# Diagonal score blocks: three quarters by matmuls, the fourth by a transposing DMA

## The chip, the core and the metric

The kernel runs on one core of one Trainium2 chip. That core has a matrix engine (TensorE, "PE" in the profile, with its weight loads shown apart as "PEld"), a vector engine (DVE), a scalar engine (ACT), GpSimd (POOL) and a queue engine (SyncE, "SP") that here issues every DMA. All DMAs of the kernel go through this one queue, in the order in which they stand there, and run on 16 DMA engines. The metric is device time in microseconds of one execution; the median of three timed runs of the kernel before is 1010.86 us (1010.35 to 1011.36).

## The reference

Two stages, on eight batches of 3136 rows:

```python
# gated attention, d_qk = 64, D = 256
scores = (1/S) * z @ z.T                 # S x S, S = 3136: symmetric
attn   = np.maximum(scores, 0.0) ** 2    # symmetric as well
x      = u * (attn @ v)
# low-rank mixer, rank 32, and a channel MLP, 256 -> 1024 -> 256
h   = x.transpose(0, 2, 1) @ U @ V
u2  = x + h.transpose(0, 2, 1)
out = u2 + np.maximum(u2 @ w_ch1, 0.0) @ w_ch2
```

The scores are a product of `z` with itself, so the block of rows J and columns g is the transpose of the block of rows g and columns J, and a block on the diagonal is its own transpose.

## The kernel before

**Tiling.** The 3136 rows of a batch are six groups of 512 rows (four tiles of 128) and one small group of 64. A score block is 512 keys by 512 queries; it is held in bf16 in one of 20 buffers (`blk0` to `blk19`) of 128 partitions by 4 x 512, with key tile `j` in columns `j*512` to `j*512+511`. For a batch there are 36 blocks. A block above the diagonal (J > g) is made once by matmuls and its mirror (rows g, columns J) is made from it by a transposing DMA. A block on the diagonal is made whole by matmuls. In batch 0 the groups 0 to 3 are an exception (`made_twice`, line 325): all of their blocks are made by matmuls.

**Making a block.** `score_pairs` (line 341) makes a block in two halves, `h` = 0 (key tiles 0 and 1) and `h` = 1 (key tiles 2 and 3). A half is a pair of matmuls, one on each half of TensorE's rows (contraction 64), each 128 keys by 512 queries, into two PSUM banks. The two matmuls of a pair run side by side. `score_finish` (line 387) has ACT or DVE apply scale and ReLU (`rectify`, line 309: one instruction of 128 x 1024, PSUM to `blk`, ACT at line 317, DVE at line 313) and then has DVE square it in place (`square`, line 307). For a block above the diagonal a transposing DMA becomes ready some time after the second square (`issue_turn`, line 328, DMA at line 333: 128 x 2048 in, 16 squares of 128 x 128 out). Among ready ones the one with the smallest J is issued first.

**Using it.** `av_stream` (line 493) runs `attn @ v` for group g over 24 key tiles, blocks 0 to 5 in order; the function `lhs` in it gives the 128 x 128 piece of a block that is the next weight. It is emitted as 96 pairs of matmuls of 256 columns, and everything else on TensorE (scores of the next group, the mixer and the MLP of a group one batch earlier) is placed between those pairs by `emit` (line 849).

**Order.** The program is written by hand, in one order, by a planner: `clock[0]` counts TensorE's work, `free_at` books ACT, DVE and the SP queue (34 units for a transposing DMA), and `hold` and `run_held` keep work until it is due by that count. So what a step costs in the planner decides where all later instructions stand on their queues. The items are the 56 (batch, group) pairs; item (b, g) runs `attn @ v` for it, makes the scores of the next group, and does the MLP of an item a batch earlier.

**The mixer's input.** For each group, `u2_unit` (line 653) makes `u2`, casts it to bf16 (`x_bf`) and has it transposed by a DMA of 128 x 1024 (`x_turn`, line 613, DMA at line 616) into `u2T`, which the first matmuls of `ch1_part` (line 745) read. This DMA stands on the same SP queue as the transposing DMAs of the score blocks, the loads of `u` (line 270), `v` (line 227) and `z` (lines 200, 205) and the stores of the output (line 824).

Of the kernel before, what the change touches and what calls it, by code (L numbers as in the profile page):

```python
# [18 lines left out]
def kernel(  # L19
# [11 lines left out]
    nc = tc.nc  # L31
# [5 lines left out]
    P = 128  # L37
# [7 lines left out]
    GW = GT * P  # L45
# [35 lines left out]
    squared = {}  # L81
    blocks = {}

    def take_block():
        k = free_blocks.pop(0)
        return k, pool.tile([P, GT, GW], BF16, name=f"blk{k}", bufs=1)
# [9 lines left out]
    clock = [0.0]  # L96
    free_at = {"act": 0.0, "dve": 0.0, "sp": 0.0}
    held = []
    unturned = {}
    ready_turns = []  # L100

    def book(eng, ready, cost):
        free_at[eng] = max(free_at[eng], ready) + cost
        return free_at[eng]

    def hold(due, f):
        held.append((due, len(held), f))

    def run_held(now=None):
        now = clock[0] if now is None else now  # L110
        while True:
            ripe = [h for h in held if h[0] <= now]
            if not ripe:
                break
            h = min(ripe, key=lambda e: (e[0], e[1]))
            held.remove(h)
            h[2]()
        while ready_turns and free_at["sp"] <= now:
            issue_turn(min(ready_turns, key=lambda e: (e[0], e[2], e[1])))

    def pe(cost):
        clock[0] += cost
# [3 lines left out]
    ps_free = [0.0] * NPS  # L126

    def take_ps():
        k = min(range(NPS), key=lambda i: ps_free[i])
        assert ps_free[k] < float("inf")  # L130
        clock[0] = max(clock[0], ps_free[k])
        ps_free[k] = float("inf")
        for bank in range(2):
            wrote.pop((k, bank), None)
        return k, ps_pool.tile([P, 2, GW], FP32, name=f"ps{k}")
# [23 lines left out]
    def pair(k, ops, n):  # L159

        if any(wrote.get((k, bank), (h,))[0] != h for h, bank, _ in ops):
            post(k)
        for h, bank, args in ops:
            ins = nc.tensor.matmul(**args)  # L164
            last = wrote.get((k, bank))
            if last and last[0] != h:
                behind(ins, last[2])
            wrote[k, bank] = [h, ins, None]
        pe(n / 256)
# [132 lines left out]
    def half(zzT, jj, c0, n):  # L302
        return zzT.rearrange("p t c -> p (t c)")[jj * dqk : (jj + 1) * dqk, c0 : c0 + n]

    def square(a, cost=6.3):
        book("dve", clock[0], cost)
        nc.vector.tensor_tensor(out=a, in0=a, in1=a, op=ALU.mult)  # L307

    def rectify(dst, src):

        ready = clock[0] + 3
        if max(free_at["dve"], ready) + 8 < max(free_at["act"], ready):
            nc.vector.tensor_scalar(  # L313
                out=dst, in0=src, scalar1=scale, scalar2=0.0, op0=ALU.mult, op1=ALU.max
            )
            return book("dve", ready, 11.2)
        nc.scalar.activation(out=dst, in_=src, func=AF.Relu, scale=scale)  # L317
        return book("act", ready, 8.7)

# [3 lines left out]
    def made_twice(b, g):  # L325
        return b == 0 and g <= FIRST

    def issue_turn(e):
        ready_turns.remove(e)
        J, g, b = e  # L330
        src = blocks[b, g, J]
        blocks[b, J, g] = take_block()
        nc.sync.dma_start_transpose(
            out=blocks[b, J, g][1].rearrange("p j (q c) -> p (j q) c", c=P),
            in_=src[1].rearrange("p j c -> p (j c)"),
        )
        book("sp", clock[0], 34)
        if unturned.pop(src[0]):
            free_blocks.append(src[0])

    def score_pairs(jobs):

        made = []
        for b, g, job in jobs:
            zzT = zzTs[b]
            k, ps = take_ps()
            if job == "last":
                keys, cols = [NF, NF], [groups[g + jj][0] for jj in range(2)]
            else:
                J, h = job  # L350
                keys, cols = [J * GT + 2 * h + jj for jj in range(2)], [groups[g][0]] * 2
            pair(
                k,
                [
                    (
                        jj,
                        jj,
                        dict(
                            out=ps[:, jj, :],
                            lhsT=half(zzT, jj, keys[jj] * P, P),  # L360
                            rhs=half(zzT, jj, cols[jj], GW),
                            start=True,
                            stop=True,
                        ),
                    )
                    for jj in range(2)
                ],
                GW,
            )
            if job == "last":  # L370
                lasts[b, g // 2] = pool.tile([P, 2, GW], BF16, name="last_sb")
                made.append((lasts[b, g // 2], k, ps, None, None))
                continue
            if h == 0:
                blocks[b, g, J] = take_block()
            made.append(
                (
                    blocks[b, g, J][1][:, 2 * h : 2 * h + 2, :],
                    k,
                    ps,  # L380
                    (J, g, b) if h == 1 and J > g and not made_twice(b, J) else None,
                    (b, g, J),
                )
            )
        return made

    def score_finish(made):
        for dst, k, ps, turn, key in made:
            if turn:
                J, g, b = turn  # L390
                unturned[blocks[b, g, J][0]] = False
            done = rectify(dst, ps)
            ps_free[k] = done

            def finish(dst=dst, turn=turn, key=key):
                square(dst)
                if key:
                    squared[key] = squared.get(key, 0) + 1
                if turn:
                    hold(clock[0] + 7, lambda: ready_turns.append(turn))  # L400

            hold(done, finish)

    def score_burst(jobs):
        score_finish(score_pairs(jobs))
# [87 lines left out]
    def av_stream(b, g, box):  # L493
        def lhs(h, q, jt):
            jb, j = divmod(jt, GT)
            while (b, jb) not in v_cast:
                if spare and not b:
                    spare.pop(0)()
                else:
                    run_held(min(h[0] for h in held))  # L500
            while (b, g, jb) not in blocks:
                if (g, jb, b) in ready_turns:
                    issue_turn((g, jb, b))
                else:
                    run_held(min(h[0] for h in held))
            t = blocks[b, g, jb][1]
            if jb >= g or made_twice(b, g):
                while squared.get((b, g, jb), 0) < 2:
                    run_held(min(h[0] for h in held))
                return t[h, j, q * P : (q + 1) * P]  # L510

            return t.rearrange("p a c -> p (a c)")[h, (q * GT + j) * P : (q * GT + j + 1) * P]

        per = 2 * GT

        def step(i, way, first, least):
            if first:
                xs[b, g] = pool.tile([P, GT, D], BF16, name="x_bf", bufs=8)
                box["k"], box["ps"] = take_ps()
            jt, a = divmod(i, 2)  # L520
            pair(
                box["k"],
                crossed(
                    way,
                    a,
                    lambda h, q: dict(
                        out=four(box["ps"])[:, q, :],
                        lhsT=lhs(h, q, jt),
                        rhs=v_bfs[b][h, jt, :],
                        start=first,  # L530
                        stop=False,
                    ),
                ),
                D,
            )
            while box.get("given", 0) < least // per:
                give_block(blocks[b, g, box.get("given", 0)])
                box["given"] = box.get("given", 0) + 1

        return Ways(2 * NF, 1, step, box)  # L540
# [487 lines left out]
    made = score_pairs(jobs_of(0, 0)[0:4])  # L1028
# [23 lines left out]
    for b in range(B):  # L1052
        for g in range(NQ):
            t = b * NG + g - 1
            new = jobs_of(b, g)
            if g == 0 and b > 0:
                x, y = (5, 10) if b == 1 else (5, 11)
# [14 lines left out]
    for t in range(n_items):  # L1072
# [45 lines left out]
        if av and full:  # L1118
# [5 lines left out]
            n = len(mine) - 3  # L1124
            qs += [(9 + 74 * i / n, 1, False, lambda: scores(1)) for i in range(n)]
        elif av:
# [5 lines left out]
            k = min(2, len(mine) // 3)  # L1132
            n = len(mine) - 3 * k
# [98 lines left out]
```

## Time and profile before

| what | value |
|---|---|
| timed runs, median | 1010.86 us (1010.35 to 1011.36) |
| the profiled execution: span from first to last instruction | 1010.2 us |
| TensorE: matmuls busy | 986.7 us, 98% of the span, 16171 matmuls |
| TensorE: weight loads busy | 776.4 us, 77% |
| DVE busy | 648.0 us, 64% |
| ACT busy | 517.3 us, 51% |
| mean granted TensorE clock | 0.997 of full speed |
| DMA queue of the kernel | 166.64 MB, 76.9% of 16 engines' span |
| transposing DMAs of score blocks | 114 (128 x 2048); beside them 55 for `u2T` and 7 for `zzT` |

The profile gives the span of its execution and no other time of it; the timed median lies 0.65 us above that span. The page's second part shows the same thing over time: TensorE's digit is 9 in every slice from the sixth to the 39th of 40 (some 25 us each) and lower only in the first, fourth, fifth and last, and the DMA row has 9 in six of the first fifteen slices. The other engines are well below full everywhere. A matmul's busy time is its latency and not the time for which it keeps the array, so pairs overlap; how long one pair keeps TensorE is read from the starts of runs of equal matmuls.

### The profile page before, as it was taken

How to read it: one execution, taken by the hardware profiler on the slowest of the kernel's cores; microseconds unless marked ns; L12 is line 12 of the kernel's file. 1: busy time of each engine (PE TensorE's matmuls, PEld its weight loads, DVE VectorE, ACT ScalarE, POOL GpSimd, SP SyncE). 2: the span in 40 equal slices, each digit the busy share in tenths (PEclk: the TensorE clock that was granted, in tenths of full speed). 3: DMA queues.
4: the chain of work that ended last, by engine and by line, in shares of the span. 5: the costliest groups of instructions: out<-in, count | busy, mean ns of one | idle time of the engine just before them, and what ended most of it. 6: DMA issues, size and time to landing. Idle time of an engine off the chain costs nothing.

```text
span 1010.2 us, 35325 instructions
## 1 busy us (share of the span) xinstructions
PE 986.7 (98%) x16171; PEld 776.4 (77%) x16171; DVE 648.0 (64%) x816; ACT 517.3 (51%) x595; POOL 17.1 (2%) x24
## 2 busy tenths in 40 slices
PE   5998899999999999999999999999999999999998
PEld 3897677777787777778777877778777777777776
DVE  4974675667656685666856677566776667653453
ACT  5885653357524574355733556434654356532453
POOL 4100000000000000000000000000000000000000
PEclk9999999999999999999999999999999999999999
DMA  7899997487976799558996689856799577953142
GB/s 242 166 249 225 218 203 165 127 171 176 224 149 159 140 204 214 150 150 174 183 215 165 130 184 190 216 127 140 179 209 191 138 152 128 180 127 88 45 103 94
DMA packets 341221, 168.89 MB, mean 167 GB/s; under 512 B 316496, under 2 KB 319568, under 8 KB 341072
## 3 DMA queue, kind: packets, MB, share of 16 engines
q1 hardware_dynamic: 341072, 166.64, 76.9%
q8 instruction: 126, 2.06, 0.9%
q14 instruction: 23, 0.19, 0.1%
HBM read 62.56 MB, written 25.69 MB: 87 GB/s over the span
## 4 chain that ended last, share of the span: by engine, by line
PE 94%; DMA 2%; ACT 1%; DVE 1%; POOL 0%; issue 0%; SPq 0%; POOLq 0%; ACTq 0%
PE ps L164 92%; PE ps L551 1%; DMA blk<-blk 1%; ACT blk L785 1%; PE ps L627 1%; DMA blk<-in_v_dram 1%; DVE blk L307 1%; ACT blk L317 1%; PE ps L835 0%; DMA u2T<-x_bf 0%; DVE blk L313 0%; POOL z_bf L213 0%; POOL v_bf L232 0%; DVE blk L822 0%; DVE x_bf L584 0%
## 5 line engine op out<-in xcount | busy, mean ns | idle before, releaser
L164 PEld LDWEIGHTS <-blk 64*128 64x128 bf16 x12288 | 611.0, 94 | 163.6 <-POOLq L154 8.8
L164 PE MATMUL ps<-v_bf,blk 64*128 64x256 bf16 x9216 | 617.2, 270 | 5.0 <-DMA blk<-blk 3.2
L317 ACT ACTIVATE blk<-ps 128x1024 bf16<-128x1024 f32 x321 | 320.7, 1028 | 342.0 <-PE ps L164 330.4
L307 DVE TENSOR_TENSOR blk<-blk 128x1024 bf16<-128x1024 bf16 x348 | 234.1, 698 | 42.2 <-ACT blk L317 41.6
L164 PE MATMUL ps<-u2T,w_bf 64*128 64x512 bf16 (+1 forms) x1792 | 237.8, 349 | 3.4 <-DMA u2T<-x_bf 2.7
L164 PE MATMUL ps<-w_bf,blk 64*128 64x256 bf16 x3072 | 193.5, 269 | 0.2
L782 DVE TENSOR_SCALAR blk<-ps 128x1024 bf16<-128x1024 f32 x94 | 113.3, 1205 | 100.0 <-PE ps L164 100.0
L785 ACT ACTIVATE blk<-ps 128x1024 bf16<-128x1024 f32 (+1 forms) x130 | 109.4, 850 | 82.4 <-PE ps L164 74.1
L164 PE MATMUL ps<-zzT 64*128 64x512 bf16 (+1 forms) x936 | 141.7, 343 | 1.7 <-ACT zzT L297 1.7
L164 PEld LDWEIGHTS <-w_bf 64*128 64x128 bf16 x1792 | 90.7, 94 | 34.6 <-POOLq L154 3.0
L584 DVE TENSOR_TENSOR x_bf<-ps,u_sb 128x1024 bf16<-128x1024 f32 x48 | 58.8, 1224 | 62.3 <-PE ps L164 62.3
L700 DVE TENSOR_TENSOR out_sb<-ps,x_bf 128x1024 f32<-128x1024 f32 (+1 forms) x49 | 54.3, 1107 | 53.4 <-PE ps L164 53.3
L822 DVE TENSOR_TENSOR out_sb<-ps,out_sb 128x1024 f32<-128x1024 f32 x42 | 51.3, 1222 | 18.3 <-PE ps L164 18.3
L164 PEld LDWEIGHTS <-zzT 64*128 64x128 bf16 x936 | 43.0, 95 | 9.3 <-ACT zzT L297 2.2
L317 ACT ACTIVATE last_sb<-ps 128x1024 bf16<-128x1024 f32 x23 | 23.6, 1024 | 26.1 <-PE ps L164 26.0
L313 DVE TENSOR_SCALAR blk<-ps 128x1024 bf16<-128x1024 f32 x23 | 28.2, 1225 | 13.4 <-PE ps L164 11.9
L186 DVE CAST x_bf<-out_sb 128x1024 bf16<-128x1024 f32 x34 | 23.4, 689 | 0.5
L164 PE MATMUL ps<-t_sb,V_bf 64*128 64x256 bf16 x200 | 20.7, 269 | 0.0
L186 DVE CAST v_bf<-stage 128x1024 bf16<-128x1024 f32 (+1 forms) x33 | 20.2, 611 | 0.0
L164 PE MATMUL ps<-v_bf,last_sb 64*128 64x256 bf16 x192 | 18.5, 269 | 0.0
L822 DVE TENSOR_TENSOR blk<-ps,blk 128x1024 f32<-128x1024 f32 x6 | 7.3, 1225 | 16.0 <-PE ps L164 15.9
L570 ACT COPY u_sb<-ps 64x512 f32<-64x512 f32 x8 | 4.7, 582 | 23.8 <-PE ps L551 23.8
(67 smaller groups left out, 248.6 us busy)
## 6 DMA issues: line engine op xcount, KB each, us to landing
u_sb<-in_u_dram SPq DMA_DIRECT2D x48, 512.0 KB, 5.0
stage<-in_v_dram SPq DMA_DIRECT2D x42, 512.0 KB, 6.0
out_dram<-out_sb SPq DMA_DIRECT2D x42, 512.0 KB, 3.1
stage<-in_z_dram SPq DMA_DIRECT2D x7, 512.0 KB, 5.7
blk<-in_v_dram SPq DMA_DIRECT2D x6, 512.0 KB, 7.3
out_dram<-blk SPq DMA_DIRECT2D x6, 512.0 KB, 2.6
blk<-in_moe_w_ch_dram SPq DMA_DIRECT2D x4, 512.0 KB, 6.6
blk<-blk SPq DMA_TRANSPOSE x114, 5.1
```

What stands on the lines that cost most here:

```text
L164: ins = nc.tensor.matmul(**args)
L186: nc.vector.tensor_copy(out=out, in_=in_)
L307: nc.vector.tensor_tensor(out=a, in0=a, in1=a, op=ALU.mult)
L313: nc.vector.tensor_scalar(out=dst, in0=src, scalar1=scale, scalar2=0.0, op0=ALU.mult, op1=ALU.max)
L317: nc.scalar.activation(out=dst, in_=src, func=AF.Relu, scale=scale)
L551: nc.tensor.matmul(out=ps[c * hp : c * hp + rows, h, :D], lhsT=smalls[b][h * hp : (h + 1) * hp, jt, :], rhs=v_bfs[b][h * hp : (h + 1) * hp ...
L584: nc.vector.tensor_tensor(out=xs[b, g][:rows, :n, :], in0=four(box["ps"])[:rows, :n, :], in1=u_sbs[b, g][:rows, :n, :], op=ALU.mult,)
L627: nc.tensor.matmul(out=pt[c * R : (c + 1) * R, 0, :D], lhsT=U_bf[:rows, it, :], rhs=xs[b, g][:rows, q, :], start=(it < NREP), stop=(it + N ...
L700: nc.vector.tensor_tensor(out=o[:rows, :n, :], in0=four(ps)[:rows, :n, :], in1=x, op=ALU.add)
L782: nc.vector.tensor_single_scalar(out=r, in_=ps[:, :, :gw], scalar=0.0, op=ALU.max)
L785: nc.scalar.activation(out=r, in_=ps[:, :, :gw], func=AF.Relu)
L822: nc.vector.tensor_tensor(out=o, in0=acc, in1=o, op=ALU.add)
```

## The change

A block on the diagonal is its own transpose. It is cut in quarters of two tiles by two tiles. The change makes the two quarters of key tiles 0 and 1, and the quarter of key tiles 2, 3 and query tiles 2, 3 by matmuls; the quarter of key tiles 2, 3 and query tiles 0, 1 is the transpose of the quarter of key tiles 0, 1 and query tiles 2, 3, and a transposing DMA of 128 x 512 makes it. So the first half (`h` = 0) is made by a pair of 512 columns as before, the second by a pair of 256 columns, and its ReLU and its square work on 512 columns per partition and not on 1024. The block's buffer keeps its size but holds the quarters in four runs of 512 columns: key tiles 0, 1 by queries 0, 1; the same by queries 2, 3 (what the DMA reads); key tiles 2, 3 by queries 2, 3; and what the DMA writes. `in_split` finds a piece there. This holds for all diagonal blocks but those that are `made_twice`: 2 in batch 0 and 6 in each of 7 batches, 44 in all.

The DMA becomes ready, by the planner, seven units after the first half's square, is booked with 12 units on the SP queue, and is chosen among the ready ones by the same rule as before (smallest J first). Where the stream of `attn @ v` comes to a piece of the fourth quarter and the DMA has not been placed yet, `lhs` places it then.

```diff
+    def split(b, g, J):
+        return J == g and not made_twice(b, g)
+    hw = GW // 2
+    def in_split(j, q):
+        if j < 2:
+            return (q // 2 * 2 + j) * hw + q % 2 * P
+        return 2 * GW + (j - 2) * hw + (q - 2) * P if q >= 2 else 3 * GW + (q * 2 + j - 2) * P
...
-            return book("dve", ready, 11.2)
+            return book("dve", ready, 11.2 if part == 1 else 6.4)
...
-        return book("act", ready, 8.7)
+        return book("act", ready, 8.7 if part == 1 else 5.3)
...
     def issue_turn(e):
         ready_turns.remove(e)
         J, g, b = e
         src = blocks[b, g, J]
+        if J == g:
+            nc.sync.dma_start_transpose(
+                out=flat_of(src)[:, 3 * GW :].rearrange("p (n c) -> p n c", c=P),
+                in_=flat_of(src)[:, GW : 2 * GW],
+            )
+            book("sp", clock[0], 12)
+            split_turned.add((b, g))
+            return
...
                 keys, cols = [J * GT + 2 * h + jj for jj in range(2)], [groups[g][0]] * 2
+                if split(b, g, J) and h:
+                    width = hw
+                    cols = [c + hw for c in cols]
...
-                            out=ps[:, jj, :],
+                            out=ps[:, jj, :width],
                             lhsT=half(zzT, jj, keys[jj] * P, P),
-                            rhs=half(zzT, jj, cols[jj], GW),
+                            rhs=half(zzT, jj, cols[jj], width),
...
+    def score_finish_split(flat, k, ps, h, key):
+        if h:
+            done = rectify(
+                flat[:, 2 * GW : 3 * GW].rearrange("p (j c) -> p j c", c=hw), ps[:, :, :hw], 0.5
+            )
+            a, cost = flat[:, 2 * GW : 3 * GW], 3.7
+        else:
+            done = rectify(
+                flat[:, : 2 * GW].rearrange("p (w j c) -> p j w c", w=2, j=2),
+                ps.rearrange("p j (w c) -> p j w c", w=2),
+            )
+            a, cost = flat[:, : 2 * GW], 6.3
+        ps_free[k] = done
+        def finish():
+            square(a, cost)
+            squared[key] = squared.get(key, 0) + 1
+            if not h:
+                b, g, J = key
+                hold(clock[0] + 7, lambda: ready_turns.append((J, g, b)))
+        hold(done, finish)
...
+                if split(b, g, jb):
+                    while j >= 2 and q < 2 and (b, g) not in split_turned:
+                        if (g, g, b) in ready_turns:
+                            issue_turn((g, g, b))
+                        else:
+                            run_held(min(h[0] for h in held))
+                    x = in_split(j, q)
+                    return t.rearrange("p a c -> p (a c)")[h, x : x + P]
                 return t[h, j, q * P : (q + 1) * P]
```

More of the change, by code (lines that the diff above doesn't have):

```diff
@@ L303, in half, with flat_of @@
         return zzT.rearrange("p t c -> p (t c)")[jj * dqk : (jj + 1) * dqk, c0 : c0 + n]
+    def split(b, g, J):
+        return J == g and not made_twice(b, g)
+    def flat_of(entry):
+        return entry[1].rearrange("p a c -> p (a c)")
+    hw = GW // 2
[3 more added lines that the diff above has]
+        return 2 * GW + (j - 2) * hw + (q - 2) * P if q >= 2 else 3 * GW + (q * 2 + j - 2) * P
     def square(a, cost=6.3):
@@ L307, in square, with rectify @@
         nc.vector.tensor_tensor(out=a, in0=a, in1=a, op=ALU.mult)
-    def rectify(dst, src):
+    def rectify(dst, src, part=1):
         ready = clock[0] + 3
-        if max(free_at["dve"], ready) + 8 < max(free_at["act"], ready):
+        if max(free_at["dve"], ready) + 8 * part < max(free_at["act"], ready):
             nc.vector.tensor_scalar(
@@ L315, in rectify @@
             )
-            return book("dve", ready, 11.2)
+            return book("dve", ready, 11.2 if part == 1 else 6.4)
         nc.scalar.activation(out=dst, in_=src, func=AF.Relu, scale=scale)
-        return book("act", ready, 8.7)
+        return book("act", ready, 8.7 if part == 1 else 5.3)
     def made_twice(b, g):
         return b == 0 and g <= FIRST
+    split_turned = set()
     def issue_turn(e):
@@ L346, in score_pairs @@
             k, ps = take_ps()
+            width = GW
             if job == "last":
@@ L367, in score_pairs @@
                 ],
-                GW,
+                width,
             )
@@ L375, in score_pairs @@
                 blocks[b, g, J] = take_block()
+            if split(b, g, J):
+                made.append((flat_of(blocks[b, g, J]), k, ps, h, (b, g, J)))
+                continue
             made.append(
@@ L388, in score_finish @@
         for dst, k, ps, turn, key in made:
+            if key and split(*key):
+                score_finish_split(dst, k, ps, turn, key)
+                continue
             if turn:
```

## The prediction

> **What bounds the kernel now.** I read the chain that ended last, then the stages, then TensorE's waits, then the queue that issues the DMAs. Chain and stages (columns: stretch, its length, busy time of PE, PEld, DVE, ACT, POOL, granted clock, DMA share, GB/s):
>
> ```profile
> PE 94%; DMA 2%; ACT 1%; DVE 1%; POOL 0%; issue 0%; SPq 0%; POOLq 0%; ACTq 0%
> ...
> 75.00:100.00 25.00, 21.81 (x369) 17.95 (x367) 12.14 (x20) 14.18 (x18) 0.00 (x0) 0.93 1.11 238
> 100.00:118.70 18.70, 18.70 (x344) 14.57 (x341) 13.33 (x21) 14.33 (x16) 0.00 (x0) 1.00 1.05 203
> 118.70:122.00 3.30, 0.67 (x14) 0.36 (x8) 3.08 (x5) 0.00 (x0) 0.00 (x0) 1.00 1.17 243
> 122.00:126.00 4.00, 3.97 (x38) 2.56 (x40) 0.00 (x0) 1.91 (x2) 0.00 (x0) 0.57 1.08 218
> 247.00:368.00 121.00, 120.91 (x2009) 95.19 (x2005) 80.56 (x102) 60.73 (x71) 0.00 (x0) 1.00 0.84 175
> 490.00:612.00 122.00, 121.91 (x2027) 95.98 (x2023) 81.57 (x104) 61.08 (x72) 0.00 (x0) 1.00 0.86 173
> ```
>
> TensorE works without a gap through a whole batch (120.91 of 121 us) at full clock: there, less matmul time is less time. Only before 126 us does it wait for DMAs, and there the DMA share is over 1. TensorE's waits between 15 and 125 us (total, times, longest):
>
> ```profile
> PE ps L164 <- DMA blk<-blk: 3.2, 1, 3.2
> PE ps L164 <- DMA u2T<-x_bf: 2.7, 1, 2.7
> ```
>
> The first ends at 81.1 us, the second at 122.0 us. What a pair of matmuls costs (start, duration, matmuls in a run):
>
> ```profile
> 279.75 1.47 PE L164 MATMUL ps<-w_bf,blk 64*128 64x256 bf16 x24
> 281.06 1.04 PE L164 MATMUL ps<-v_bf,blk 64*128 64x256 bf16 x16
> ...
> 126.10 0.38 PE L164 MATMUL ps<-zzT 64*128 64x512 bf16 x2
> 126.32 0.59 PE L164 MATMUL ps<-u2T,w_bf 64*128 64x512 bf16 x4
> ```
>
> Four more pairs of 256 columns take 1.47 - 1.04 = 0.43 us, 0.107 each; one more pair of 512 takes 0.59 - 0.38 = 0.21. The SP queue (start, duration), first before the second wait, then in a later batch:
>
> ```profile
> 85.34 0.46 SPq L227 DMA_DIRECT2D stage<-in_v_dram  x1
> 89.79 3.47 SPq L333 DMA_TRANSPOSE blk<-blk  x1
> 93.36 0.54 SPq L275 DMA_DIRECT2D u_sb<-in_u_dram  x1
> 93.98 0.54 SPq L227 DMA_DIRECT2D stage<-in_v_dram  x1
> 94.61 7.29 SPq L333 DMA_TRANSPOSE blk<-blk  x2
> 103.78 0.34 SPq L270 DMA_DIRECT2D u_sb<-in_u_dram  x1
> ...
> 356.33 1.24 SPq L200 DMA_DIRECT2D stage<-in_v_dram  x2
> 358.76 3.03 SPq L333 DMA_TRANSPOSE blk<-blk  x1
> 361.88 1.26 SPq L616 DMA_TRANSPOSE u2T<-x_bf  x1
> 365.98 0.50 SPq L824 DMA_DIRECT2D out_dram<-out_sb  x1
> ```
>
> From 69.9 to 122 us the queue stands still only at 85.80-89.79 (4.0 us) and 101.90-103.78 (1.9 us). Price of a transposing DMA on the queue, by its two lines (min/median/max in ns):
>
> ```profile
> L333 SPq DMA_TRANSPOSE blk<-blk x114: 1316/2802/7607, 24.4 to 904.3; - x114
> L616 SPq DMA_TRANSPOSE u2T<-x_bf x55: 1158/1261/2318, 118.7 to 988.8; - x55
> ```
>
> **The change part by part.** *Removed on TensorE:* 44 pairs shrink from 512 to 256 columns: 44 x (0.21 - 0.107) = 44 x 0.107 = 4.7 us (the 512 pair is twice the 256 pair within the reading). The other way to read it, by mean durations (382 against 270 ns), gives 44 x 0.112 = 4.9; I take 4.7. The built order of TensorE is otherwise the same: no matmul or weight load is added. A pair of 256 columns is what the stream of attn @ v already runs at 0.107 with two weight loads of 94 ns in it, so the loads don't eat the gain. Four of the 44 pairs stand ahead of the wait that ends at 122.0; time saved ahead of a wait for a DMA only lengthens the wait. 40 x 0.107 = 4.3 us count.
>
> *ACT and DVE:* 44 ReLUs and 44 squares work on half the columns. They are faster (ACT's 128x512 form takes 606 ns against 1028 for 128x1024), but TensorE waits for neither engine after 35 us, and no diagonal is split before that: worth 0. The first half's ReLU writes two runs per bank instead of one; I price that between 0 and 0.2 us each on engines that are 64% and 51% busy: 0 on the path.
>
> *Added on SP:* 44 transposing DMAs of 128x512, a quarter of L333's bytes and half of L616's. No row shows this size. From below: 2.80 / 4 = 0.70 us, if a full queue moves by bytes. From above: 2.80, as a whole block. I take 1.25, L616's median, whose smallest is 1.16: it is the nearest by size, and a kind that hardly follows its bytes. A rule of the Trainium skill speaks against the change: by "VectorE: DVE Perf Modes", section "The three transpose paths", a 128x128 square costs 1309 ns by DMA against 390 on TensorE. A quarter of four squares would be an estimated 5.2 us by it, and the four below some 21 us; but L333's 16 squares leave the queue in 2.8 us, and so the trace doesn't bear that price.
>
> Each quarter waits for its square on DVE, and whatever stands behind it on SP waits too: loads of u and v, whole blocks, and the u2T that TensorE needs next. Its own reader is far off: in the built order at least 11 us of matmuls lie between the place of a quarter and the first weight load from it. It is u2T that comes late.
>
> *At the start:* four quarters stand ahead of the u2T of 122.0 us: one behind the second whole block of 69.9-83.6, two ahead of the block of 89.79, one between the last two blocks before 118.68. The first three, 3 x 1.25 = 3.75 us, go into the 4.0 us of the standing queue. The fourth has no cover: 1.25 us. The DMA engines have little idle time there (share 1.1), so some bytes of the three drain later: 0.25 more. u2T lands 1.5 us later (between 0.3, by 0.70 with part hidden, and 5, with nothing hidden), and the 2.65 us wait becomes 2.65 + 0.43 + 1.5 = 4.6. The first wait, 81.1 us, is for a block issued ahead of any quarter: unchanged.
>
> The clock: after the 2.65 us wait it is 0.57 over 122-126 us. I count the same loss after a wait of 4.6. "TensorE: Matmul & The Clock Gate", Part 1, of the Trainium skill has the clock halve only after a window of 3.4 us without work; by that rule 2.65 would not have tripped it and 4.6 newly would, an estimated 1.7 us more. The trace disagrees: it tripped already, so I add 0.
>
> *In the batches:* six quarters each. By landing times in the trace, u2T has little to spare three times in a batch. At the first place (367.04 us in the batch shown) it lands 1.6, 1.0, 0.7, 1.9, 2.1, 1.3 us before its first use over six batches; at the third 1.4, 1.2, 0.4, 3.1, 1.5, 1.8. Ahead of both a quarter is added. At the first place in the two tightest batches the queue stands still for 1.2 us (357.57-358.76) just where the quarter goes: covered, and 0.8 us in sum if not. At the third, 1.25 late costs 0.9 + 0.1. At the second (0.3 to 2.5 to spare) a quarter is added as well, but a whole block moves ahead of the store of 365.98, into 2.8 us of idle queue, which also relieves the third. I take 0.5 us in all (between 0 and 3).
>
> *Sum:* the profile's span, 1010.2, and 0.65 around it are the median of 1010.86. 1010.86 - 4.3 + 1.5 + 0.5 = 1008.6.
>
> **The rivals.**
> - *All DMAs hidden.* The queue waits for data or stands idle for some 50 of a batch's 122 us, and quarters fit there. Against it: no idle behind 103.78. No added wait: 1010.86 - 4.3 = 1006.6.
> - *The start eats most of it.* Between 75 and 119 us the DMA share is 1.05 to 1.11, so a standing queue is not idle engines: three of four quarters count, 3 x 1.25 = 3.75, and 0.5 in the batches: 1010.8, no change. For it: the loads issued before 85.8 land until 93.7.
> - *Slower: u2T late in each batch.* If a quarter costs 2.0 on SP (L616's max is 2.3, L333's median 2.8) and the idle doesn't help, the spares above leave waits of 3.4 us at the first places and 3.8 at the third ones, and 2.5 at the start: 1010.86 - 4.3 + 9.7 = 1016.3. It decides from about 1.45 us a quarter, where the waits equal 4.3. The skill's price per square would push the same way. Against it: L616 is 1.26 in the median, and squares four times as many as a quarter's leave in 1.32 when the queue is free.
>
> That the pairs don't shrink is excluded by the built order.
>
> **How the numbers follow.** Forecast 0.40 (own range 1007.4 to 1010.0), hidden 0.20, eaten at the start 0.22, slower 0.18. A measurement of this kernel tells about 0.2%, 2.0 us, from no change: faster means below 1008.8. Hidden (0.20) and some 0.65 of the forecast's case (0.26) give 0.46; the rest of it and most of the second rival 0.35; slower 0.19. Range 1006.2 to 1013.0: down to the hidden case, up through the second and the near end of the third.
>
> **What would show it.** TensorE's zzT group would hold 88 matmuls of 64x256. The quarter's own line on SP would have a median near 1.25 and nothing of TensorE waiting for it. The wait for u2T<-x_bf at 122 would be some 4.6 us; a batch would last 0.6 us less (121.0). I am wrong if u2T waits appear in every batch, or if the quarter's line is over 1.45.

## The result, and the profile after

| what | before | after |
|---|---|---|
| median of runs taken in turn on one chip | 1011.36 us (1008.68 to 1012.91, 21 runs) | 1012.89 us (1011.26 to 1019.16, 21 runs) |
| ratio, 95% interval | | 1.0023 [1.0014, 1.0031] |
| second comparison, with the experiments | 1011.45 us (25 runs) | 1011.36 us (12 runs), ratio 1.0002 [0.9991, 1.0014] |
| profiled execution: span, granted clock | 1010.2 us, 0.997 | 1017.4 us, 0.992 |
| second profiled execution of after | | 1009.5 us, 0.994 |

The change took 4.7 us of matmuls away and gained nothing: 0.23% slower in one comparison, no change in the other, whose interval touches the first. The first profile of after is of its slowest execution (1019.16 us; the time lies some 1.8 us above the span in these runs). The second is of one near its median (1011.22 us). So the first shows the added waits at their largest; the second shows them in an ordinary execution, and is the only one of that kind.

The chain that ended last, in the profile of after, by engine:

```profile
PE 89%; DMA 6%; DVE 2%; ACT 1%; SPq 1%; issue 1%; POOL 0%; POOLq 0%; ACTq 0%
```

Before, DMAs held 2% of it. TensorE's waits, by what ended them (in all, times, longest), in after, and then in its second profile:

```profile
PE ps L164 <- DMA u2T<-x_bf: 12.6, 8, 5.4
...
PE ps L164 <- DMA blk<-blk: 3.3, 1, 3.3
```

```profile
PE ps L164 <- DMA u2T<-x_bf: 6.3, 3, 5.1
```

The wait for `u2T` was 2.7 us, once. It is now 5.1 to 5.4 us at the start, and beside it there are waits in the batches: seven with 12.6 - 5.4 = 7.2 us in the first profile, two with 1.2 in the second. Of the 7.2 us, 4.9 are at the third `u2T` of a batch, 1.9 at the first and 0.4 at the second. No line of TensorE waits for the quarter itself, in either. The stretches of after that answer to those of before (busy time of PE, PEld, DVE, ACT, POOL, granted clock, DMA share, GB/s):

```profile
118.00:123.00 5.00, 0.00 (x0) 0.00 (x0) 2.07 (x3) 0.00 (x0) 0.00 (x0) 0.76 1.11 208
123.00:127.40 4.40, 4.33 (x36) 2.62 (x38) 0.00 (x0) 1.76 (x2) 0.00 (x0) 0.50 1.07 239
127.40:131.00 3.60, 3.60 (x54) 2.43 (x52) 2.45 (x4) 3.31 (x6) 0.00 (x0) 1.00 1.11 255
...
488.00:611.00 123.00, 122.49 (x2051) 97.91 (x2049) 81.08 (x105) 60.12 (x73) 0.00 (x0) 1.00 0.93 179
```

TensorE does nothing at all from 118 to 123 us, then runs at a clock of 0.50 until 127.4. The batch shown last has 0.51 us without TensorE, where a batch of before had 0.09, and the DMA share has gone from 0.86 to 0.93.

What the change did to its own pieces is as it should be. TensorE's score matmuls by shape in after (count, busy us, mean ns, idle before):

```profile
L164 PE MATMUL ps<-zzT 64*128 64x512 bf16 x656 | 122.4, 383 | 1.7 <-ACT zzT L297 1.7
...
L164 PE MATMUL ps<-zzT 64*128 64x256 bf16 x88 | 12.2, 272 | 0.0
```

And the quarter's line on SP (duration in ns, min/median/max, first and last start; then from issue to landing):

```profile
L349 SPq DMA_TRANSPOSE blk<-blk x44: 1188/1207/2217, 79.4 to 923.1; - x44
...
DMA to landing us min/median/max: 2.5/4.6/8.2
```

To compare executions whose beginnings differ by chance (the first wait, for `blk<-blk`, ends between 77.0 and 81.1 us, whatever the kernel), I cut each trace at three points that every kernel has: the end of that first wait, the first matmul that reads `u2T`, and TensorE's last. The start is the first stretch, the batches are the second:

| kernel | start, us | batches, us |
|---|---|---|
| before | 40.95 | 883.4 |
| after | 43.48 | 889.3 |
| after, second profile | 43.19 | 881.5 |

The start got 2.2 to 2.5 us longer, although 0.43 us of its matmuls are gone. The batches, which should have lost 4.3 us, lost 1.9 in one execution and gained 5.9 in the other; about 1.5 of these 5.9 us are half clock behind one of the waits (shown below, at 411.09 us).

### The profile page after: what moved, and what is told of

It reads as the page before. It is cut to its first block, busy times and chain, and to the rows that moved or that the text cites. A ratio compares the mean times of both kernels' runs of the same rounds, so it can differ in the third digit from the quotient of the medians.

```text
span 1017.4 us, 35440 instructions
## 1 busy us (share of the span) xinstructions
PE 984.4 (97%) x16171; PEld 780.7 (77%) x16171; DVE 635.9 (63%) x821; ACT 500.5 (49%) x590; POOL 17.2 (2%) x24
## 4 chain that ended last, share of the span: by engine, by line
PE 89%; DMA 6%; DVE 2%; ACT 1%; SPq 1%; issue 1%; POOL 0%; POOLq 0%; ACTq 0%
PE ps L164 86%; DMA u2T<-x_bf 4%; PE ps L616 1%; DMA blk<-blk 1%; ACT blk L850 1%; DVE blk L321 1%; DMA stage<-in_z_dram 1%; PE ps L692 1%; SPq L357 1%; DMA blk<-in_v_dram 1%; ACT blk L331 1%; PE ps L900 0%; POOL z_bf L213 0%; DVE blk L327 0%; SPq L205 0%
## 5 line engine op out<-in xcount | busy, mean ns | idle before, releaser
L331 ACT ACTIVATE blk<-ps 128x1024 bf16<-128x1024 f32 (+1 forms) x327 | 306.6, 969 | 358.4 <-PE ps L164 351.9
L321 DVE TENSOR_TENSOR blk<-blk 128x1024 bf16<-128x1024 bf16 x348 | 222.3, 667 | 50.0 <-ACT blk L331 49.5
L164 PE MATMUL ps<-u2T,w_bf 64*128 64x512 bf16 (+1 forms) x1792 | 238.8, 351 | 13.3 <-DMA u2T<-x_bf 12.6
L847 DVE TENSOR_SCALAR blk<-ps 128x1024 bf16<-128x1024 f32 (+1 forms) x111 | 122.8, 1106 | 109.6 <-PE ps L164 109.0
L850 ACT ACTIVATE blk<-ps 128x1024 bf16<-128x1024 f32 (+1 forms) x113 | 101.0, 903 | 86.6 <-PE ps L164 79.2
L164 PE MATMUL ps<-zzT 64*128 64x512 bf16 (+2 forms) x936 | 137.1, 333 | 1.7 <-ACT zzT L297 1.7
L327 DVE TENSOR_SCALAR blk<-ps 128x1024 bf16<-128x1024 f32 x17 | 20.8, 1225 | 7.3 <-PE ps L164 5.7
L186 DVE CAST x_bf<-out_sb 128x1024 bf16<-128x1024 f32 x30 | 20.7, 690 | 0.5
L321 DVE TENSOR_TENSOR last_sb<-last_sb 128x1024 bf16<-128x1024 bf16 x24 | 16.4, 683 | 0.2 <-ACT last_sb L331 0.2
```

The lines of the kernel that those rows point to most:

```text
L186: nc.vector.tensor_copy(out=out, in_=in_)
L327: nc.vector.tensor_scalar(out=dst, in0=src, scalar1=scale, scalar2=0.0, op0=ALU.mult, op1=ALU.max)
L847: nc.vector.tensor_single_scalar(out=r, in_=ps[:, :, :gw], scalar=0.0, op=ALU.max)
L850: nc.scalar.activation(out=r, in_=ps[:, :, :gw], func=AF.Relu)
```

## The experiments

Two theories stood against each other. *Queue:* the saving is real, and the quarter's place on the SP queue ahead of `u2T` gives it back, at the start and in the batches. *No saving:* the smaller pairs save less than counted, or the extra bytes slow all transfers, wherever the quarter stands. Diffs are against the changed kernel. Ratios are against the kernel before, with 95% intervals.

**The saving without the DMA.** The transposing DMA is left out, and `attn @ v` reads the untransposed quarter in its place (so those scores are not the reference's); TensorE, ACT and DVE keep their order.

```diff
-        return 2 * GW + (j - 2) * hw + (q - 2) * P if q >= 2 else 3 * GW + (q * 2 + j - 2) * P
+        return 2 * GW + (j - 2) * hw + (q - 2) * P if q >= 2 else GW + (q * 2 + j - 2) * P
...
-            nc.sync.dma_start_transpose(
-                out=flat_of(src)[:, 3 * GW :].rearrange("p (n c) -> p n c", c=P),
-                in_=flat_of(src)[:, GW : 2 * GW],
-            )
```

> The 44 quarter DMAs are left out and the planner's booking of them is kept, so that TensorE, DVE and ACT have the same instructions in the same order as in the changed kernel; the stream reads the untransposed quarter in its place, so its values there are not the reference's. Theory Q (the quarter DMA on the SP queue makes the u2T of TensorE's next matmuls late): the wait at 121 us goes back from 5.4 to some 3 us, the waits for u2T in the batches (6.9 us in seven waits) vanish, and the time is the one before less the saved matmuls that count, 1011.4 - 4.3 = 1007.1. Theory O (not the DMA but the changed order, 12 booked units, moved whole blocks and other engines for ReLU, makes u2T late): the waits stay and the time stays at 1012 to 1013.

Measured: 0.9963 [0.9948, 0.9977]. Start 41.25 us, batches 878.9: 883.4 - 878.9 = 4.5 us less, against 4.3 counted. TensorE's only wait for `u2T` is that of the start; then two batches of this kernel:

```profile
PE ps L164 <- DMA u2T<-x_bf: 3.2, 1, 3.2
...
240.00:361.00 121.00, 120.91 (x2019) 96.61 (x2017) 79.66 (x105) 58.70 (x71) 0.00 (x0) 1.00 0.84 174
361.00:482.00 121.00, 120.91 (x2019) 96.66 (x2017) 79.65 (x105) 58.70 (x71) 0.00 (x0) 1.00 0.83 175
```

One batch is 121.0 us (the same counts and busy times of TensorE repeat after 121 us), and TensorE is idle for 0.09 of it. The saving is there in full when no quarter stands on the queue.

**A quarter of the bytes, the same place.** The DMA moves one square of 128 x 128 and not four; pieces of the other three are read untransposed (again not the reference's scores).

```diff
-        return 2 * GW + (j - 2) * hw + (q - 2) * P if q >= 2 else 3 * GW + (q * 2 + j - 2) * P
+        return 2 * GW + (j - 2) * hw + (q - 2) * P if q >= 2 else 3 * GW if q * 2 + j == 2 else GW + (q * 2 + j - 2) * P
...
-                out=flat_of(src)[:, 3 * GW :].rearrange("p (n c) -> p n c", c=P),
-                in_=flat_of(src)[:, GW : 2 * GW],
+                out=flat_of(src)[:, 3 * GW : 3 * GW + P].rearrange("p (n c) -> p n c", c=P),
+                in_=flat_of(src)[:, GW : GW + P],
```

> As the change, but the quarter DMA moves one square of 128x128 and not four (three of four pieces are then read untransposed, not the reference's values). If the price is the place on the queue (1.2 us of issue, which hardly follows the bytes): its line still has a median of 1.15 to 1.2 us, waits for u2T remain in the batches, and the time is 1011 to 1013. If the price is the bytes on the DMA engines (a quarter of them is left): the time comes within 1 us of the kernel without the quarter DMA, some 1008.

Measured: 1.0004 [0.9993, 1.0015]; start 43.65 us, batches 882.2. The DMA's line, and TensorE's wait:

```profile
L349 SPq DMA_TRANSPOSE blk<-blk x44: 1106/1172/2022, 78.6 to 915.2; - x44
```

```profile
PE ps L164 <- DMA u2T<-x_bf: 7.3, 5, 5.6
```

With a quarter of the bytes the DMA occupies SP for 1172 ns instead of 1207, and the time is that of the change, not that of the kernel without the DMA. So what costs is that such a DMA stands there, and not its bytes.

**No quarter at the start.** The blocks (0,4), (0,5), (1,0) and (1,1), written as (batch, group), are made whole as before; 40 stay split.

```diff
-        return J == g and not made_twice(b, g)
+        return J == g and b >= 1 and not (b == 1 and g <= 1)
```

> The four diagonals whose quarter stands ahead of the wait at 121 us (batch 0, groups 4 and 5; batch 1, groups 0 and 1) are made whole; 40 are split. Theory Q: the wait at the start is 2.7 us again with 3.4 us of half clock after it and not 6.8; that is worth 1.0 us of place plus some 1 to 1.7 us of clock: 1012.9 - 2.3 = 1010.6; waits in the batches remain. If the start is not where the loss arises: no change from 1012.9.

> None split at the start, all due times as in the change, once more: its first profiled execution had hardly a wait for u2T in the batches (0.4 us) and was the fastest of its runs, so it didn't show what the median of 1.0002 is made of. Theory Q: ratio 0.999 to 1.001 again, and waits for u2T in the batches of this profile in proportion to its span, up to some 4 us, at the first, second or third u2T of a batch. If the ratio falls to that of the version with later due times, the due times don't matter.

Measured: 1.0002 [0.9990, 1.0014] and 1.0002 [0.9990, 1.0013]. The start is back to 40.8 and 41.8 us, and still nothing is gained. The batches took 879.9 us in one profile and 883.9 in the other:

```profile
PE ps L164 <- DMA u2T<-x_bf: 6.2, 7, 3.6
```

That is the second one: a wait of 3.6 us at the start and six waits in the batches with 2.6 us. By the ratios the batches alone eat the gain of 4.3 us; the prediction gave them 0.5. The traces show only part of that. The first is of the fastest execution of its set (1007.55 us, median 1011.32). In the second, an estimated 1.2 us of the 883.9 are no price of a quarter but the clock: after the wait at the start it is at half for 5.8 us of the batches (121.80 to 127.58 us), where before has 3.4. In the eight traces without a quarter at the start this wait is 2.4 to 3.6 us, with the same order on SP up to there.

**Quarters only where the queue has been seen idle.** Groups 0, 4 and 5 are split, without (1,0): 20 blocks, none ahead of a `u2T` that is needed soon.

```diff
-        return J == g and not made_twice(b, g)
+        return J == g and g in (0, 4, 5) and b >= 1 and (b, g) != (1, 0)
```

> Only diagonals whose quarter falls where the SP queue is idle and no u2T is next are split: groups 0, 4 and 5 of a batch, none ahead of the wait at the start: 20 of the 44. Theory Q: no wait for u2T in the batches, the start as before, and 20 x 0.107 = 2.1 us saved: 1011.4 - 2.1 = 1009.3. Theory O (order and bookings): the waits appear here too, since the planner moves things for these as well, and the time is at or over 1011.4.

> The 20 splits in idle places, once more: 20 x 0.107 = 2.1 us and no waits give 0.998 (first measured 0.9995, 0.9981 to 1.0009). If it stays at 0.9995 or above, these quarters cost something that no wait for u2T shows.

Measured: 0.9995 [0.9981, 1.0009] and 0.9989 [0.9981, 0.9998]. In both traces the only wait for `u2T` is that of the start (2.6 and 2.5 us), and the batches took 881.7 us, 1.8 less than before: 20 x 0.107 = 2.1 was to be had. The ratios show less of it, 0.5 and 1.1 us, and the whole of it, a ratio of 0.9979, lies just outside both intervals. A small gain is likely; what takes the rest isn't shown.

**The change again, beside the DMA without the saving.** The changed kernel once more, unaltered, and in the same set a kernel that makes the second half's pair with all 512 columns (the planner's cost stays that of 256, so the order on the engines is the same) and uses the right half of the result.

```diff
-            width = GW
+            width = cost = GW
...
                 if split(b, g, J) and h:
-                    width = hw
-                    cols = [c + hw for c in cols]
+                    cost = hw
...
-                width,
+                cost,
...
-                flat[:, 2 * GW : 3 * GW].rearrange("p (j c) -> p j c", c=hw), ps[:, :, :hw], 0.5
+                flat[:, 2 * GW : 3 * GW].rearrange("p (j c) -> p j c", c=hw), ps[:, :, hw:], 0.5
```

> The changed kernel once more, unaltered, beside the others of this set: a ratio of about 1.002 to the kernel before, and a second profile of it. The first profiled execution was the slowest of 21 (1019.2 us); in this one the waits for u2T in the batches should be shorter than its 6.9 us in sum, the wait at 121 us again about 5.4 us with 6.8 us of half clock behind it.

> As the change, but the second half's pair keeps 512 columns, so that the 44 quarter DMAs are paid and no matmul time is saved (half of each such product is not used). If saving and price simply add up: the changed kernel's 1.002 + 4.3/1011 = 1.0066. If waits for u2T take up TensorE's time (theory Q: a slower TensorE is waited for less), part of the 4.3 us is hidden in waits that shorten: 1.004 to 1.006.

Measured: the change 1.0002 [0.9991, 1.0014], without the saving 1.0040 [1.0024, 1.0056]. The difference is 0.0038, 3.8 us, of the 4.7 taken off TensorE; with these intervals it can't be told from 4.3. So the smaller pairs save about what they should also in the presence of the DMAs, and the DMAs alone cost some 4 us (1.0024 to 1.0056: 2.4 to 5.7). The profile of this kernel is of its slowest execution (1020.01 us): start 44.3 us, batches 888.2.

**The same quarters, behind `u2T`.** As in the kernel without quarters at the start, but the planner lets the quarters of groups 1, 2 and 3 become ready 38, 58 and 62 units later, which puts them, or a whole block in their stead, behind the `u2T` that they stood ahead of. Bytes, DMAs and matmuls are the same as in that kernel.

```diff
-        return J == g and not made_twice(b, g)
+        return J == g and b >= 1 and not (b == 1 and g <= 1)
...
-                hold(clock[0] + 7, lambda: ready_turns.append((J, g, b)))
+                hold(clock[0] + 7 + {1: 38, 2: 58, 3: 62}.get(g, 0), lambda: ready_turns.append((J, g, b)))
```

> None of the four at the start is split, and in groups 1 to 3 the quarter becomes ready 38, 58 and 62 planner units later, so that it, or a whole block in its stead, stands behind the next u2T on the SP queue; 40 splits. Theory Q (a quarter or what it displaces ahead of u2T makes it late): no waits for u2T in the batches, the start as before, and 40 x 0.107 = 4.3 us saved: ratio 0.9958 to 0.997. If the load on the DMA engines sets it and not the place in the queue: as the kernel with none at the start, 1.000.

> The version with none split at the start and the quarters of groups 1 to 3 due later, once more beside the next three: theory Q, ratio 0.9956 to 0.997 to the kernel before, and faster than the kernel that differs from it in the due times alone by 3 to 5 us.

Measured: 0.9956 [0.9942, 0.9971] and 0.9968 [0.9955, 0.9980]. The two kernels differ in due times alone, and the time differs by 1.0002 - 0.9956 = 0.0046 and 1.0002 - 0.9968 = 0.0034: 3.4 to 4.6 us. (Only the second pair was measured in one set, where the medians are 1010.76 and 1007.35 us; the first lies across two.) Batches 880.3 and 879.6 us. TensorE's waits for `u2T` in the second:

```profile
PE ps L164 <- DMA u2T<-x_bf: 2.8, 2, 2.4
```

What the place does is seen on SP in the same part of the fourth batch (start, duration). The changed kernel, first profile:

```profile
385.74 5.37 SPq L357 DMA_TRANSPOSE blk<-blk  x2
391.21 0.60 SPq L889 DMA_DIRECT2D out_dram<-out_sb  x1
391.86 0.44 SPq L270 DMA_DIRECT2D u_sb<-in_u_dram  x1
392.34 0.94 SPq L227 DMA_DIRECT2D stage<-in_v_dram  x1
393.33 8.52 SPq L280 DMA_TRANSPOSE zzT<-z_bf  x1
401.95 1.20 SPq L349 DMA_TRANSPOSE blk<-blk  x1
403.27 4.17 SPq L357 DMA_TRANSPOSE blk<-blk  x1
407.81 1.25 SPq L681 DMA_TRANSPOSE u2T<-x_bf  x1
```

The kernel without the quarter's DMA:

```profile
383.40 0.88 SPq L227 DMA_DIRECT2D stage<-in_v_dram  x1
384.33 6.04 SPq L280 DMA_TRANSPOSE zzT<-z_bf  x1
391.65 2.53 SPq L353 DMA_TRANSPOSE blk<-blk  x1
394.23 1.32 SPq L677 DMA_TRANSPOSE u2T<-x_bf  x1
```

The kernel with the quarters behind `u2T`, second profile:

```profile
387.34 7.55 SPq L280 DMA_TRANSPOSE zzT<-z_bf  x1
394.99 1.21 SPq L349 DMA_TRANSPOSE blk<-blk  x1
396.30 1.26 SPq L681 DMA_TRANSPOSE u2T<-x_bf  x1
397.66 5.22 SPq L357 DMA_TRANSPOSE blk<-blk  x2
```

In the first, each instruction up to the whole block at 403.27 starts within 0.12 us of the end of the last one: for 21.7 us the queue has no gap, and then 0.37 us ahead of `u2T`. Without quarters it has one (384.33 + 6.04 = 390.37, and the next starts at 391.65). And the quarter isn't alone in being longer: `zzT` takes 8.52 us and not 6.04, the whole block 4.17 and not 2.53. TensorE pays at the end of it (in brackets the idle time before the matmul, and what ended it; then the stretch behind the wait, in the columns of the stretches above):

```profile
411.09 1.03 PE L164 MATMUL ps<-u2T,w_bf 64*128 64x512 bf16 x4 [2.68 <-DMA u2T<-x_bf]
...
411.09:414.10 3.01, 3.01 (x24) 1.65 (x26) 0.00 (x0) 0.44 (x1) 0.00 (x0) 0.50 1.12 289
```

The wait has a second price: the 3.01 us behind it run at a granted clock of 0.50, an estimated 1.5 us lost. In the third the quarter at 394.99 still stands ahead of `u2T`, but the other quarter now stands behind the second `u2T` and one whole block behind this one, and `u2T` starts 8.96 us after `zzT` does, against 14.48 in the changed kernel and 9.90 without quarters.

The same over five batches, from a batch's store just behind its first `u2T` to its third `u2T`, in the mean (the rest of a length is the 0.05 us between two instructions). The last column says when the stretch begins, against the moment at which TensorE is ready for the first `u2T`:

| kernel | on SP in this stretch | its length, us | SP at work | SP idle | begins, us |
|---|---|---|---|---|---|
| before | 7 whole blocks | 34.6 | 32.7 | 0.6 | -1.1 |
| no quarters' DMAs | 6 whole blocks | 32.6 | 29.2 | 2.2 | -0.7 to -0.1 |
| after, second profile | 6 whole blocks, 2 quarters | 35.1 | 33.2 | 0.6 | -0.6 to 0.0 |
| after, first profile | 6 whole blocks, 2 quarters | 35.8 | 34.2 | 0.3 | -0.3 to 1.2 |
| none at the start, two profiles | 6 whole blocks, 2 quarters | 34.5, 35.1 | 32.6, 33.6 | 0.5, 0.2 | -0.6 to 0.8 |
| behind `u2T`, two profiles | 6 whole blocks, 2 quarters | 34.7, 34.3 | 33.3, 32.8 | 0.1, 0.2 | -1.5 to -1.0 |

The queue was full in this stretch before the change already. The change moves one whole block out of it, to ahead of the store, which makes room; two quarters then take 4.0 us in the milder case, 33.2 - 29.2: 2.0 us each, of which 1.2 is a quarter's own line and the rest that of the others, which get longer. So the stretch begins and ends later than before, while TensorE arrives earlier.

The last two rows differ in due times alone. The stretch holds as much in both and is about as long; what the later due times change is its beginning, some 1.3 us earlier, since less stands ahead of the store (in the batch shown one whole block fewer, which stands behind the third `u2T` instead). The third `u2T` then lands 0 to 2.8 us before its use in these five batches, and 0 to 0.9 without them.

**Quarters only at the start.** The counterpart: just the four blocks of the start are split.

```diff
-        return J == g and not made_twice(b, g)
+        return J == g and (b, g) in ((0, 4), (0, 5), (1, 0), (1, 1))
```

> Only the four diagonals ahead of the wait at 121 us are split, in the queue order that the change has there; 40 are made whole. Theory Q with the start as the larger part: the wait is 5.4 us and not 2.7, with 6.8 us of half clock behind it: 1.0 us of place, 1.0 to 1.7 us of clock, so + 2.0 to 2.7 us, ratio 1.002 to 1.0027. If the start costs only its place: 1.001.

Measured: 1.0018 [1.0006, 1.0031]; start 42.1 us, and one wait:

```profile
PE ps L164 <- DMA u2T<-x_bf: 5.7, 1, 5.7
```

The start costs 1.8 us [0.6, 3.1] by the ratio, 1.2 by this trace (2.2 to 2.5 in those of the change). In this trace alone the clock stays full behind the first wait, where all others have half clock for 3.4 us or more; so TensorE comes earlier to the second one, and the 5.7 us are not quite like the 5.1 to 5.4 of the change. With 1.0002 for the batches the two halves make 1.0020, next to the 1.0023 of the first comparison, but not to the 1.0002 of the second.

**All 44 split, with the later due times.** Later due times for batch 1 from group 2 on, and for all later batches; the start is as in the change.

```diff
-                hold(clock[0] + 7, lambda: ready_turns.append((J, g, b)))
+                hold(clock[0] + 7 + {1: 38, 2: 58, 3: 62}.get(g if b > 1 or (b == 1 and g > 1) else 0, 0), lambda: ready_turns.append((J, g, b)))
```

> All 44 are split, in the change's queue order up to the wait at 121 us and with the later due times in the batches behind it. Theory Q: the gain of the version with later due times less the price of the start, 0.9960 + 0.0018 = 0.998; in the profile a wait of some 5.5 us at 121 us with 6.8 us of half clock, and hardly any in the batches. If start and batches are not independent: 1.000 or above.

Measured: 0.9971 [0.9959, 0.9983]; start 42.7 us, batches 881.0. Later due times alone turn the change from no gain to a gain of 0.29%. It should have been some 0.2% behind the kernel that leaves the start alone; it is 0.03% behind it in the same set, and the intervals (0.9959 to 0.9983 against 0.9955 to 0.9980) can't tell.

**The best version** is the one with the quarters behind `u2T` and none at the start: 1007.53 and 1007.35 us, 3 to 4 us faster than both kernels.

## Why the prediction was wrong, step by step

The forecast was 1008.6 us, 0.2% faster; measured were 1012.89 and 1011.36. The step that failed is the price of a quarter ahead of `u2T`: it was counted as its own line, 1.25 us, of which idle time of the queue nearby was taken off.

- **Removed on TensorE, 4.7 us, 4.3 of it counting:** right. The batches without quarters' DMAs lose 4.5 us; the kernel with the DMAs but without the saving is 3.8 us behind the change.
- **0.65 us around the span:** misread, without harm to the forecast, which is a difference to the median. The result's runs have some 1.8 us outside of the span, so the profiled execution of before took about 1012.0 us and not 1010.86.
- **88 matmuls of 64 x 256, a batch of 121.0 us:** the shape is there, and 121.0 us is what a batch without waits takes.
- **ACT and DVE at nothing:** right. In all of after TensorE waits 1.7 us for ACT's `zzT`, as before, and 1.8 us for DVE's squares, as before.
- **1.25 us for a quarter on SP:** right as a price of the line alone (1.207). It was taken to be the whole price, and that is the error below.
- **The start, +1.5 us, wait of 4.6:** mis-sized. The wait is 5.1 to 5.4 us, and the start, from the first wait to the first use of `u2T`, grew by 2.2 to 2.5 where 4.6 - 2.65 - 0.43 = 1.5 was expected. In the other kernels with these four quarters the wait is 4.6 to 5.7 us. The step that failed is that three quarters go into the standing queue. SP in after, in the place of the idle 85.80 to 89.79:

```profile
84.70 0.45 SPq L227 DMA_DIRECT2D stage<-in_v_dram  x1
85.25 2.88 SPq L349 DMA_TRANSPOSE blk<-blk  x2
88.23 5.40 SPq L357 DMA_TRANSPOSE blk<-blk  x1
```

  Two quarters do fit there, but the block behind them takes 5.40 us instead of 3.47 and ends 14.0 us after the end of the first wait, not 12.2. The standing queue hid the instructions and not the transfers: the second rival's argument, that a standing queue is not idle engines, held for about half of their price.
- **The clock, no further loss:** about right. The trace's record of the clock has it at half for 6.83 us (120.56 to 127.38) where it was 3.41, but half of that now falls in the longer wait: the matmuls under half clock are those from 123.07 to 127.38, 4.3 us, against 122.58 to 126.00, 3.4; at half speed the difference costs 0.45 us. By the clock-gate rule weighed in the prediction ("TensorE: Matmul & The Clock Gate", Part 1, of the Trainium skill) the longer wait newly costs an estimated 1.7; the runs don't show that, since a wait of 2.65 us had already set the clock to half. What the prediction left out is the clock in the batches: in the first profile of after, the wait that ends at 411.09 us brought 3.01 us at half clock, about 1.5 us of price.
- **In the batches, +0.5 us:** this is the step that failed most. The due times alone are worth 3.4 to 4.6 us by the ratios, so that is what quarters ahead of `u2T` cost there; the waits in single traces are smaller. I priced each quarter at its own place, with its own 1.25 us, against the time that the `u2T` behind it had to spare, and called the idle 1.2 us ahead of it a cover. But from behind the first to the third `u2T` of a batch the queue stood idle for only 0.6 us in 34.6. Two quarters stand in that stretch, their lengths add up, and they lengthen the others: 4.0 us in sum, more than the whole block that moves out of it gives back. That block and a quarter also stand ahead of it now, so that it begins later. The third `u2T` lands 1.8 to 3.2 us before its use without quarters (six batches), and 0 to 2.0 us before it in the two profiles of the change. At the first `u2T` the quarter is not all of it: even without quarters' DMAs it lands only 0 to 1.0 us before its use, where it was 0.7 to 2.1 before the change.
- **The rivals.** "All hidden" fell: it needs the waits not to grow. "The start eats most of it" had the right result for the wrong reason; with no quarters at the start the gain is still gone. "Slower: `u2T` late in each batch" had the right mechanism and, with 2.0 us a quarter, the right price. It put this price on the quarter's own line, which is 1.2, and so its mark, 1.45 us on that line, missed it. It asked for 3.4 + 3.8 = 7.2 us of waits in the batches: the first profile of after has 7.2, the second 1.2, and the medians lie below that rival's 1016.3 us. The equal sum is luck: it lies at 4.9 at the third `u2T` and 1.9 at the first. The prediction's own mark, that it is wrong if `u2T` waits appear in every batch, came near to true in the first profile of after (seven waits, in five batches); the second has waits in two.

**What stays open.** Two comparisons of the same change gave 1.0023 and 1.0002; neither is a gain, but the size of the loss, between nothing and 0.3%, isn't settled. The waits in the batches vary between executions of one kernel (7.2 and 1.2 us for the change, 0.4 and 2.6 without quarters at the start), and what sets them off isn't shown. So no trace shows the whole of what the medians lose in the batches. What the four quarters at the start cost isn't settled either: 1.8 us alone, but next to nothing between the two kernels with later due times. That a full queue makes the other transposing DMAs longer is read from their lines; why, is not tried.

## What to carry to other kernels

A matmul that is traded for a DMA is paid for by what stands behind that DMA in its queue: sum the queue's work over the whole stretch up to the next transfer that the critical engine needs, and compare it with the idle time of that stretch, not with the idle time beside each new instruction. Ask also what moves ahead of that stretch, since it then begins later. Idle time of a queue was no full cover here where transfers ahead of it were still under way (a block behind two quarters took 5.40 us and not 3.47). When such a DMA is not needed soon itself, put it behind the urgent one: here its place alone was worth 3.4 to 4.6 us of 1010, and its bytes next to nothing.

## What the runs showed of the hardware that was not expected

- A transposing DMA's time on its queue hardly depends on its size when it is small: 1172 ns for one square of 128 x 128, 1207 for four, 1279 for `u2T`'s eight in the median (longest 2557).
- Transposing DMAs that stand in a full queue take longer on it. The median of the seven `zzT` transfers is 6.1 us without the quarters' DMAs, and 7.1 and 6.6 in the two profiles of the change (6.6 before, with a whole block more in the stretch); a whole block behind two quarters took 5.40 us where it had taken 3.47.
- What sets TensorE's clock to half is not the length of a wait alone. In the clock records of all 14 profiles the times at half clock that lie between 40 us and the end of the batches are 3.41 or 6.83 us long, and within a trace they start at whole multiples of 3.413 us from each other. Cut into windows on this raster, every window at full clock with 2.23 us or more without a matmul is followed by one at half clock, and none with 1.56 us or less. So a wait of 2.40 us (quarters behind `u2T`, at the start) brought 3.41 us at half clock, while the first wait of 2.71 us in the kernel with quarters only at the start, of which 1.15 us lie in one window and 1.56 in the next, brought none.
